# Words of a float64 weight landing in the memory of the other weight, loaded ahead of their rounding

## The chip, the core and the metric

The kernel runs on one core of a Trainium2 chip. The metric is device time in microseconds (us), the median of several executions. TensorE (PE) multiplies matrices, VectorE (DVE) and ScalarE (ACT) work elementwise, SyncE (SP) issues the loads and GpSimd (POOL) the stores. Each engine takes its own instructions strictly in the order in which the program wrote them, and waits for the others by semaphores.

## The reference, cut to what matters

```
B, H, S, Ns, D = 8, 8, 512, 32, 64            # x: (B,H,S,D), state: (B,H,Ns,D), float32
scores  = scale * x @ state^T                  # per batch and head
xread   = softmax(scores) @ state
scores2 = scale * state @ x^T
sread   = softmax(scores2) @ x
t   = concat([xread, sread], axis=2)           # (B,H,544,64) -> (B*544, 512)
h   = t @ w_in                                 # w_in: (512, 2048), float64
g   = h * sigmoid(1.702 * h)
out = g @ w_out                                # w_out: (2048, 512), float64 -> float32
```

Both weights arrive as float64, 8.4 MB each, and the kernel has to round them to float32 itself.

## The kernel before, in words

**Rounding the weights.** The two weights are cut into 32 pieces of 128 rows by 512 float64 numbers (512 KB of words each): pieces 0 to 15 are w_in (four column chunks c of four row blocks k), pieces 16 to 31 are w_out (block f). `load_weight` (L116) brings the words of a piece into a buffer `raw`, of which the pool has three. `round_a` (L142) makes a power of two from the exponent bits: one DVE instruction (L147) and two of ACT (L148, L149). `round_b` (L151) has four DVE instructions (L158 to L161) and writes the float32 piece; it needs the power. `round_next` (L167) does round_a up to two pieces ahead, then one round_b, and then issues the load of the piece three after the one just rounded, since its buffer is now free. A w_in piece is loaded as two transfers of 64 partitions, because heads j and j+4 are paired and their rows of w_in are not neighbours; a chunk c of x takes two transfers for the same reason.

**The batches.** For batch b: `att_state` and `att_xT` transpose state and x on PE with copies on ACT; `att_scores` makes the scores; `att_read_scores`, `att_x_exp`, `att_s_softmax` and `att_x_norm` are the softmaxes on DVE and ACT; `att_eT` and `att_sread` read x by state. `att_M(b, c)` (L269) multiplies state into column chunk c of w_in and needs its four pieces; ACT copies the result M out of PSUM. `up_x(b, f)` (L338) makes 128 of the 2048 columns of h and g (4 PE instructions, then one ACT activation, the gelu); `down` (L352) adds block f of w_out into the output (8 PE instructions for the four token chunks of a batch).

**The order.** All is written out by hand at L368 to L453. First batch 0 and the scores of batch 1, with the first four pieces rounded in between; then `chunk(b, c)`, which is one M and four ups, for (0,0), (0,1), (1,0), (1,1), (0,2), (0,3), most with one piece rounded after each up; then for f = 0 to 15 the down of batch 0 together with the second half of the ups of batch 1, again with one piece after each f. This is called the front below. After it come batches 1 to 7, which need no rounding.

The ups take turns in two PSUM buffers, so an up waits for the gelu of the up before last. PSUM for M, transposes and sread is also two buffers.

Of the kernel before, what the change touches and what calls it, by code (L numbers as in the profile page):

```python
# [10 lines left out]
FP32 = mybir.dt.float32  # L11
I32 = mybir.dt.int32
# [8 lines left out]
def kernel(  # L21
# [26 lines left out]
    nc = tc.nc  # L48

    B, H, S, D = x.shape  # L50
    Ns = state.shape[2]
    DM = H * D
    DF = moe_w_in.shape[1]
    P = 128
    NPR = P // Ns
    NG = H // NPR
    NF = DF // P
    SCH = S // P
    ST = S + Ns
    FC = 512  # L60
    NFC = DF // FC
# [4 lines left out]

    out_x = out.rearrange("(b t) n -> b t n", b=B)[:, :S].rearrange("b (c q) n -> b c q n", c=SCH)
    out_s = out.rearrange("(b t) n -> b t n", b=B)[:, S:]
    x_v = x.rearrange("b (g j) (c q) d -> b c g q j d", g=NG, c=SCH)
    st_v = state.rearrange("b (g j) n d -> b (j n) g d", g=NG)  # L70

    konst = ctx.enter_context(tc.tile_pool(name="konst", bufs=1))
    xpool = ctx.enter_context(tc.tile_pool(name="xpool", bufs=2))
    apool = ctx.enter_context(tc.tile_pool(name="apool", bufs=1))
    mpool = ctx.enter_context(tc.tile_pool(name="mpool", bufs=3))
    wpool = ctx.enter_context(tc.tile_pool(name="wpool", bufs=2))
# [15 lines left out]
    xn, stn = {}, {}  # L92

    def load_state(b):
        stn[b] = apool.tile([P, NG, D], FP32, tag="stn", name=f"stn_{b}", bufs=2)
        nc.sync.dma_start(stn[b], st_v[b])

    def load_x(b):
        xn[b] = xpool.tile([P, SCH, NPR, NG, D], FP32, tag="xn", name=f"xn_{b}")
        for c in range(SCH):  # L100
            for g in range(NG):
                nc.sync.dma_start(xn[b][:, c, :, g], x_v[b, c, g])  # L102

    def x_heads(b, c, j):
        return xn[b][:, c, j].rearrange("q g d -> q (g d)")


    w_in = [konst.tile([P, NPR, FC], FP32, name=f"w_in_{c}") for c in range(NFC)]
    w_out = [konst.tile([P, DM], FP32, name=f"w_out_{f}") for f in range(NF)]
    w_in_words, w_out_words = moe_w_in.bitcast(I32), moe_w_out.bitcast(I32)  # L110
    w_in_rows = w_in_words.rearrange("(g j d) n -> j g d n", g=NG, j=NPR)

    PIECES = [("i", c, k) for c in range(NFC) for k in range(NPR)] + [("o", f) for f in range(NF)]
    raw, power = {}, {}

    def load_weight(i):  # L116
        key = PIECES[i]
        raw[i] = wpool.tile([P, 2 * FC], I32, tag="raw", name="raw_" + "_".join(map(str, key)), bufs=3)
        if key[0] == "i":
            _, c, k = key  # L120
            for g in range(NG):
                nc.sync.dma_start(raw[i][D * g : D * (g + 1)], w_in_rows[k, g, :, 2 * FC * c : 2 * FC * (c + 1)])  # L122
        else:
            f = key[1]
            nc.sync.dma_start(raw[i], w_out_words[P * f : P * (f + 1)])

# [9 lines left out]
    def words(i):  # L138
        w = raw[i].rearrange("p (n w) -> p w n", w=2)
        return w[:, 0].bitcast(U32), w[:, 1]  # L140

    def round_a(i):  # L142

        _, hi = words(i)
        sc = wpool.tile([P, FC], I32, tag="sc", name=f"sc_{i}", bufs=3)
        power[i] = sc
        nc.vector.tensor_scalar(sc, hi, 0x7FF00000, None, ALU.bitwise_and)  # L147
        nc.scalar.activation(out=sc.bitcast(FP32), in_=sc, func=AF.Relu, bias=edge[0], scale=-8.0)  # L148
        nc.scalar.activation(out=sc, in_=sc.bitcast(FP32), func=AF.Relu, bias=edge[1], scale=-1.0)  # L149

    def round_b(i):  # L151
        key = PIECES[i]
        dst = w_in[key[1]][:, key[2]] if key[0] == "i" else w_out[key[1]]
        lo, hi = words(i)
        sc = power.pop(i)

        fr = wpool.tile([P, FC], I32, tag="fr", name=f"fr_{i}")
        nc.vector.tensor_scalar(fr, hi, 0xFFFFF, 0x100000, ALU.bitwise_and, ALU.bitwise_or)  # L158
        nc.vector.scalar_tensor_tensor(sc, hi, -0x80000000, sc, ALU.bitwise_and, ALU.bitwise_or)  # L159
        nc.vector.scalar_tensor_tensor(dst, lo, 2.0**-32, fr, ALU.mult, ALU.add)  # L160
        nc.vector.scalar_tensor_tensor(dst, dst, 2.0**-20, sc.bitcast(FP32), ALU.mult, ALU.mult)  # L161
        del raw[i]

    AHEAD = 2
    done = {"a": 0, "b": 0}

    def round_next(n):  # L167

        for _ in range(n):
            if done["b"] == len(PIECES):  # L170
                return
            while done["a"] < min(done["b"] + 1 + AHEAD, len(PIECES)):
                round_a(done["a"])
                done["a"] += 1
            round_b(done["b"])
            done["b"] += 1
            nxt = done["b"] + 2
            if nxt < len(PIECES):
                load_weight(nxt)

    def w_in_of(k, f):
        c, o = divmod(P * f, FC)
# [12 lines left out]
    def att_state(b):  # L195
        ps = att_ps([P, P], f"stT_{b}")
        nc.tensor.transpose(ps, stn[b].rearrange("p g d -> p (g d)"), ident)  # L197
        A[b]["stT"] = apool.tile([P, P], FP32, tag="stT", name=f"stT_{b}", bufs=2)
        copies(b, 0)(A[b]["stT"], ps)  # L199
# [16 lines left out]
    def att_scores(b):  # L216
        a = A[b]
        a["s"] = [psO.tile([P, S], FP32, tag="o", name=f"s_{b}_{g}") for g in range(NG)]
        by_state(b, a["s"], lambda rows, j: a["xT"][rows, j])
# [17 lines left out]
    def att_s_softmax(b):  # L237

        for e, sm in A[b]["e2"]:
            nc.vector.tensor_scalar(sm, sm, eps, None, ALU.add)  # L240
            nc.vector.reciprocal(out=sm, in_=sm)
            nc.vector.tensor_scalar(e, e, sm, None, ALU.mult)
# [3 lines left out]
    def att_x_exp(b):  # L246

        a = A[b]
        t = a["e1"].rearrange("p g i n -> p (g i) n")
        mx = apool.tile([P, NS1], FP32, tag="mx", name=f"mx_{b}")  # L250
        nc.vector.reduce_max(out=mx, in_=t, axis=AX.X)
        nc.vector.tensor_tensor(out=t, in0=t, in1=mx.to_broadcast((P, NS1, Ns)), op=ALU.subtract)
        nc.scalar.activation(out=t, in_=t, func=AF.Exp, scale=scale)

    def att_x_norm(b):

        a = A[b]
        t = a["e1"].rearrange("p g i n -> p (g i) n")
        sm = apool.tile([P, NS1], FP32, tag="sm", name=f"sm_{b}")
        nc.vector.reduce_sum(out=sm, in_=t, axis=AX.X)  # L260
        nc.vector.tensor_scalar(sm, sm, eps, None, ALU.add)
        nc.vector.reciprocal(out=sm, in_=sm)
        nc.vector.tensor_tensor(out=t, in0=t, in1=sm.to_broadcast((P, NS1, Ns)), op=ALU.mult)
        a["aT"] = apool.tile([P, NG, S], FP32, tag="aT", name=f"aT_{b}", bufs=2)
        nc.vector.transpose(
            a["aT"].rearrange("p g t -> p (g t)"), a["e1"].rearrange("p g i n -> p (g i n)")
        )
# [59 lines left out]
    G = {}  # L327
# [24 lines left out]
    def down(key, r, fs, dst):  # L352

        if fs[0] == 0:
            O[key, r] = psO.tile([P, DM], FP32, tag="o", name=f"o_{key}_{r}")
        ops = O[key, r]
        for f in fs:
            nc.tensor.matmul(  # L358
                ops, G[key, f][:, P * r : P * (r + 1)], w_out[f], start=(f == 0), stop=(f == NF - 1)
            )  # L360
        if fs[-1] == NF - 1:
            osb = opool.tile([P, DM], FP32, tag="osb", name=f"osb_{key}_{r}")
            nc.scalar.copy(osb, ops)  # L363
            nc.gpsimd.dma_start(dst, osb)  # L364

    load_state(0)  # L368
    load_weight(0)
    load_x(0)  # L370
    load_weight(1)
    load_state(1)
    load_weight(2)
    load_x(1)
    att_state(0)
    round_next(1)
    for j in range(NPR):
        att_xT(0, j)
    att_scores(0)
    att_read_scores(0)  # L380
    round_next(1)
    att_x_exp(0)
    att_s_softmax(0)
    att_x_norm(0)
    att_state(1)
    for j in range(NPR):
        att_xT(1, j)
    att_scores(1)
    for g in range(NG):
        att_eT(0, g)  # L390
    att_sread(0)
    round_next(NPR - 2)


    nper = FC // P

    def chunk(b, c, rounds):
        att_M(b, c)
        for f in range(nper * c, nper * (c + 1)):
            up_x(b, f)  # L400
            if rounds:
                round_next(1)

    chunk(0, 0, True)
    att_read_scores(1)
    att_x_exp(1)
    att_s_softmax(1)
    att_x_norm(1)
    chunk(0, 1, True)
    for g in range(NG):  # L410
        att_eT(1, g)
    att_sread(1)
    chunk(1, 0, False)
    chunk(1, 1, True)
    chunk(0, 2, True)
    chunk(0, 3, True)
    load_state(2)
    load_x(2)


    rest = list(range(2 * nper, NF))
    for f in range(NF):
        for r in range(SCH):
            down(0, r, [f], out_x[0, r])
        if f % 2:
            if rest[0] % nper == 0:
                att_M(1, rest[0] // nper)
            up_x(1, rest.pop(0))
        round_next(1)

    nb = P // Ns
    for b in range(1, B):
        ahead = b + 1 < B
# [12 lines left out]
        for u in range(4 * SCH):  # L446
            r, i = divmod(u, 4)
# [36 lines left out]
```

## Time and profile before

| | us |
|---|---|
| median of 3 runs | 945.84 (944.11 to 946.02) |
| the profiled execution | 946.34 |
| its span in the profile | 944.6 |
| PE busy | 844.3 |
| DVE busy | 203.1 |
| ACT busy | 229.1 |

The page's second part cuts the span into 40 slices of 23.6 us and gives each engine's busy share in tenths; the clock that PE was granted is given the same way. PE's busy time has modelled ends, so where it is dense the time between the starts of its instructions is the better measure. The chain of waits goes from the last instruction back to what released each step.

### The profile page before, as it was taken

How to read it: one execution, taken by the hardware profiler on the slowest of the kernel's cores; microseconds unless marked ns; L12 is line 12 of the kernel's file. 1: busy time of each engine (PE TensorE's matmuls, PEld its weight loads, DVE VectorE, ACT ScalarE, POOL GpSimd, SP SyncE). 2: the span in 40 equal slices, each digit the busy share in tenths (PEclk: the TensorE clock that was granted, in tenths of full speed). 3: DMA queues.
4: the chain of work that ended last, by engine and by line, in shares of the span. 5: the costliest groups of instructions: out<-in, count | busy, mean ns of one | idle time of the engine just before them, and what ended most of it. 6: DMA issues, size and time to landing. Idle time of an engine off the chain costs nothing.

```text
span 944.6 us, 6837 instructions
## 1 busy us (share of the span) xinstructions
PE 844.3 (89%) x2824; PEld 392.2 (42%) x2824; DVE 203.1 (22%) x366; ACT 229.1 (24%) x380; POOL 19.7 (2%) x42
## 2 busy tenths in 40 slices
PE   2555384689999999999999999999999999999997
PEld 1312331234443544354435443544354435844443
DVE  1737424444014001500050005000500050000000
ACT  3444244332102130213021302131213121202100
POOL 0000000000000000000000000000000000000000
PEclk9786587889999999999999999999999999999999
DMA  9131212353000200020002000200000000000000
GB/s 183 45 84 50 71 62 99 106 133 70 29 30 12 67 1 14 12 67 0 15 12 67 1 14 12 67 0 12 12 22 1 12 11 20 4 12 12 0 23 23
DMA packets 43967, 35.05 MB, mean 37 GB/s; under 512 B 37664, under 2 KB 37664, under 8 KB 43936
## 3 DMA queue, kind: packets, MB, share of 16 engines
q1 hardware_dynamic: 40832, 25.70, 11.0%
q0 software_dynamic: 3104, 8.92, 2.6%
q8 instruction: 22, 0.36, 0.2%
q14 instruction: 9, 0.07, 0.0%
HBM read 25.69 MB, written 8.91 MB: 37 GB/s over the span
## 4 chain that ended last, share of the span: by engine, by line
issue 66%; PE 15%; DMA 8%; DVE 6%; POOL 2%; SPq 1%; ACT 1%; POOLq 0%; DVEq 0%; ACTq 0%
PE o L358 10%; DMA raw_i<-in_moe_w_in_dram 4%; DMA raw_o<-in_moe_w_out_dram 4%; PE h L333 3%; POOL out_dram L364 2%; DVE sc L159 1%; DVE sc L147 1%; PE M L214 1%; DVE w_in L160 1%; PE sr L293 1%; SPq L122 1%; DVE fr L158 1%; SPq L102 1%; DVE w_out L160 1%; PE xT L206 0%
## 5 line engine op out<-in xcount | busy, mean ns | idle before, releaser
L358 PE MATMUL o<-w_out,g 128*128 128x512 f32 x1024 | 456.2, 595 | 0.0
L358 PEld LDWEIGHTS o<-w_out,g 128*128 128x128 f32 x1024 | 189.0, 190 | 232.8 <-issue 232.1
L333 PE MATMUL h<-aT,M 128*128 128x512 f32 x512 | 233.6, 612 | 35.0 <-ACT M L276 35.0
L333 PEld LDWEIGHTS h<-aT,M 128*128 128x128 f32 x512 | 98.9, 196 | 169.4 <-issue 115.0
L335 ACT ACTIVATE g<-h 128x512 f32<-128x512 f32 x128 | 76.1, 595 | 141.1 <-PE h L333 141.1
L214 PE MATMUL M<-w_in,stT 64*32 64x512 f32 x512 | 45.0, 622 | 16.4 <-DVE w_in L161 16.4
L276 DVE COPY M<-M 128x512 f32<-128x512 f32 x24 | 16.4, 682 | 194.6 <-PE M L214 194.6
L363 ACT COPY osb<-o 128x512 f32<-128x512 f32 x32 | 18.7, 585 | 135.2 <-PE o L358 132.9
L293 PE MATMUL sr<-eT,xn 128*128 128x64 f32 x256 | 33.0, 292 | 18.5 <-ACT eT L286 18.5
L148 ACT ACTIVATE sc<-sc,edge 128x512 f32<-128x512 int32 x32 | 23.0, 720 | 81.3 <-DVE sc L147 81.2
L206 PE MATMUL xT<-ident,xn 128*128 128x128 f32 x128 | 22.9, 310 | 21.9 <-ACT stT L199 8.1
L293 PEld LDWEIGHTS sr<-eT,xn 128*128 128x128 f32 x256 | 32.9, 209 | 21.9 <-ACT eT L286 19.0
L276 ACT COPY M<-M 128x512 f32<-128x512 f32 x40 | 22.5, 584 | 68.2 <-PE M L214 68.2
L364 POOL DMA_DIRECT2D out_dram<-osb x32 | 17.5, 546 | 866.4 <-ACT osb L363 866.3
L206 PEld LDWEIGHTS xT<-ident,xn 128*128 128x128 f32 x128 | 18.2, 161 | 36.5 <-issue 14.6
L207 ACT COPY xT<-xT 128x512 f32<-128x512 f32 x20 | 11.6, 584 | 88.3 <-PE xT L206 88.3
L333 PE MATMUL h_sr<-srT,w_in 128*128 128x256 f32 x128 | 27.8, 379 | 0.0
L358 PE MATMUL o_sr<-w_out,g_sr 128*128 128x512 f32 x64 | 27.6, 592 | 0.0
L199 DVE COPY stT<-stT 128x128 f32<-128x128 f32 x6 | 1.7, 291 | 119.8 <-PE stT L197 119.8
L214 PEld LDWEIGHTS M<-w_in,stT 64*32 64x32 f32 x512 | 7.5, 106 | 46.1 <-issue 22.7
L333 PEld LDWEIGHTS h_sr<-srT,w_in 128*128 128x128 f32 x128 | 24.3, 190 | 3.7 <-issue 0.5
L149 ACT ACTIVATE sc<-sc,edge 128x512 int32<-128x512 f32 x32 | 23.1, 722 | 1.1
(52 smaller groups left out, 306.0 us busy)
## 6 DMA issues: line engine op xcount, KB each, us to landing
raw_i<-in_moe_w_in_dram SPq DMA_DIRECT2D x32, 256.0 KB, 4.2
xn<-in_x_dram SPq DMA_DIRECT2D x64, 128.0 KB, 3.4
raw_o<-in_moe_w_out_dram SPq DMA_DIRECT2D x16, 512.0 KB, 3.3
out_dram<-osb POOLq DMA_DIRECT2D x32, 256.0 KB, 2.3
stn<-in_state_dram SPq DMA_DIRECT2D x8, 64.0 KB, 2.0
out_dram<-osb_sr POOLq DMA_DIRECT2D x2, 256.0 KB, 7.1
```

What stands on the lines that cost most here:

```text
L148: nc.scalar.activation(out=sc.bitcast(FP32), in_=sc, func=AF.Relu, bias=edge[0], scale=-8.0)
L149: nc.scalar.activation(out=sc, in_=sc.bitcast(FP32), func=AF.Relu, bias=edge[1], scale=-1.0)
L160: nc.vector.scalar_tensor_tensor(dst, lo, 2.0**-32, fr, ALU.mult, ALU.add)
L206: nc.tensor.transpose(ps[:, c], x_heads(b, c, j), ident)
L214: nc.tensor.matmul(ps[g][st], A[b]["stT"][rows, st], rhs(rows, j), start=True, stop=True)
L276: copies(b, g)(m[:, g], ps[g])
L293: nc.tensor.matmul(ps[:, j], x_heads(b, c, j), a["eT"][:, :, c, Ns * j : Ns * (j + 1)], start=(c == 0), stop=(c == SCH - 1),)
L333: nc.tensor.matmul(hps, lhs[i], rhs[i], start=(i == 0), stop=(i == n - 1))
L335: nc.scalar.activation(out=gt, in_=hps, func=AF.Gelu_apprx_sigmoid)
L358: nc.tensor.matmul(ops, G[key, f][:, P * r : P * (r + 1)], w_out[f], start=(f == 0), stop=(f == NF - 1))
L363: nc.scalar.copy(osb, ops)
L364: nc.gpsimd.dma_start(dst, osb)
```

## The change

Order and memory of the front change; no arithmetic is added or left out.

- Heads 2j and 2j+1 are paired, so a w_in piece and a chunk of x are one transfer each (x: 4 instead of 8 per batch); state becomes two transfers.
- w_out becomes one tile of 16 blocks. The words of pieces 0 to 7 land in it (two blocks hold one piece), and those of pieces 12 to 15 again in its first eight blocks. Pieces 8 to 11 and all of w_out use the pool, now with four buffers.
- Loads are issued apart from the rounding: eight pieces at the start, and from the fifth rounded piece on eight ahead of the rounding (`load_weights`, `powers_to`, `round_to`).
- The order of the first batches: fewer powers ahead at the start, `att_x_norm(0)` after the scores of batch 1; in the chunks `pace` spreads the pieces: one per up in chunk (0,0), none in (0,1), three per chunk in the next four, then 1.5 per f.

```diff
-    x_v = x.rearrange("b (g j) (c q) d -> b c g q j d", g=NG, c=SCH)
+    x_v = x.rearrange("b h (c q) d -> b c q h d", c=SCH)
...
-    w_out = [konst.tile([P, DM], FP32, name=f"w_out_{f}") for f in range(NF)]
+    w_out = konst.tile([P, NF, DM], FP32, name="w_out")
...
+        nin, room = NFC * NPR, NF // 2
+        if i < room or nin - NPR <= i < nin:
+            o = 2 * (i % room if i < room else i - (nin - NPR))
+            raw[i] = w_out[:, o : o + 2].rearrange("p f n -> p (f n)").bitcast(I32)
+        else:
+            raw[i] = wpool.tile([P, 2 * FC], I32, tag="raw", name="raw_" + "_".join(map(str, key)), bufs=4)
...
+    def powers_to(n):
+        while done["a"] < min(n, len(PIECES)):
+            load_weights(done["a"] + 1)
+            round_a(done["a"])
+            done["a"] += 1
+    def round_to(n, ahead=AHEAD):
+        while done["b"] < min(n, len(PIECES)):
+            powers_to(done["b"] + 1 + ahead)
+            round_b(done["b"])
+            done["b"] += 1
+            if done["b"] > NPR:
+                load_weights(done["b"] + 2 * NPR)
+    def pace(pieces):
+        done["credit"] += pieces
+        n = int(done["credit"])
+        done["credit"] -= n
+        round_to(done["b"] + n)
...
-    chunk(0, 1, True)
+    chunk(0, 1, 0)
...
-    chunk(1, 0, False)
-    chunk(1, 1, True)
-    chunk(0, 2, True)
-    chunk(0, 3, True)
+    chunk(1, 0, 3)
+    chunk(1, 1, 3)
+    chunk(0, 2, 3)
+    chunk(0, 3, 3)
```

SP's queue at the start of the program, before and then after (`raw_i` is the pool's buffer of a w_in piece, `xn` and `stn` are x and state of one batch):

```order
L96 DMA stn_117<-in_state_dram 128x2x64
L122 DMA raw_i_0_119<-in_moe_w_in_dram 64x1024 x2
L102 DMA xn_122<-in_x_dram 128x4x64 x8
L122 DMA raw_i_1_131<-in_moe_w_in_dram 64x1024 x2
L96 DMA stn_134<-in_state_dram 128x2x64
L122 DMA raw_i_2_136<-in_moe_w_in_dram 64x1024 x2
L102 DMA xn_139<-in_x_dram 128x4x64 x8
L122 DMA raw_i_3_169<-in_moe_w_in_dram 64x1024 x2
```

```order
L129 DMA w_out<-in_moe_w_in_dram 128x1024
L97 DMA stn_103<-in_state_dram 128x1x64 x2
L102 DMA xn_106<-in_x_dram 128x8x64 x4
L129 DMA w_out<-in_moe_w_in_dram 128x1024 x3
L97 DMA stn_114<-in_state_dram 128x1x64 x2
L102 DMA xn_117<-in_x_dram 128x8x64 x4
L129 DMA w_out<-in_moe_w_in_dram 128x1024 x4
L129 DMA raw_i_0_339<-in_moe_w_in_dram 128x1024
L129 DMA raw_i_1_341<-in_moe_w_in_dram 128x1024
L129 DMA raw_i_2_343<-in_moe_w_in_dram 128x1024
L129 DMA raw_i_3_345<-in_moe_w_in_dram 128x1024
```

The fourth piece had to wait for the first to be rounded; now eleven pieces stand behind the first with no rounding between them.

ACT at the start, before and then after (`sc` is a power, `stT` and `xT` the transposed state and x of batch 0):

```order
L199 COPY stT_150<-stT_148 128x128
L148 ACTIVATE sc_152<-sc_152,edge_112 128x512
L149 ACTIVATE sc_152<-sc_152,edge_114 128x512
L148 ACTIVATE sc_156<-sc_156,edge_112 128x512
L149 ACTIVATE sc_156<-sc_156,edge_114 128x512
L148 ACTIVATE sc_160<-sc_160,edge_112 128x512
L149 ACTIVATE sc_160<-sc_160,edge_114 128x512
L207 COPY xT_172<-xT_0_173 128x512
L207 COPY xT_172<-xT_1_179 128x512
```

```order
L152 ACTIVATE sc_126<-sc_126,edge_97 128x512
L153 ACTIVATE sc_126<-sc_126,edge_99 128x512
L216 COPY stT_137<-stT_135 128x128
L224 COPY xT_139<-xT_0_140 128x512
L224 COPY xT_139<-xT_1_146 128x512
```

The powers of pieces 1 and 2 stood ahead of the copies of batch 0's transposes; now only that of piece 0 does.

ACT in chunk (1,0), before and then after (`M` is the product of state and w_in, `g` the gelu of an up):

```order
L276 COPY M_0_572<-M_0_0_573 128x512
L276 COPY M_0_572<-M_0_1_574 128x512
L335 ACTIVATE g_0_588<-h_0_585 128x512
L335 ACTIVATE g_1_593<-h_1_590 128x512
L335 ACTIVATE g_2_598<-h_2_595 128x512
L335 ACTIVATE g_3_603<-h_3_600 128x512
L276 COPY M_1_605<-M_1_0_606 128x512
L276 COPY M_1_605<-M_1_1_607 128x512
```

```order
L293 COPY M_0_490<-M_0_0_491 128x512
L293 COPY M_0_490<-M_0_1_492 128x512
L352 ACTIVATE g_0_506<-h_0_503 128x512
L352 ACTIVATE g_1_511<-h_1_508 128x512
L152 ACTIVATE sc_513<-sc_513,edge_97 128x512
L153 ACTIVATE sc_513<-sc_513,edge_99 128x512
L352 ACTIVATE g_2_527<-h_2_524 128x512
L152 ACTIVATE sc_529<-sc_529,edge_97 128x512
L153 ACTIVATE sc_529<-sc_529,edge_99 128x512
L352 ACTIVATE g_3_543<-h_3_540 128x512
L152 ACTIVATE sc_545<-sc_545,edge_97 128x512
L153 ACTIVATE sc_545<-sc_545,edge_99 128x512
```

Three powers now stand among the four gelus of this chunk, the last of them ahead of the copies of the next M.

## Rows read from the trace of the kernel before

**Rows 1.** The page, 40 slices of the span: PE's busy share in tenths.

```profile
PE   2555384689999999999999999999999999999997
```

**Rows 2.** Busy time by stretch: span, us and instructions of each engine, granted clock, DMA share, GB/s.

```profile
120.70:258.20 137.50, 108.85 (x305) 45.44 (x306) 49.80 (x93) 45.48 (x73) 1.22 (x2) 0.90 0.28 81
258.20:944.60 686.40, 680.88 (x2295) 318.97 (x2293) 96.73 (x168) 138.64 (x234) 17.71 (x32) 1.00 0.06 19
```

**Rows 3.** The chain of waits, a w_in piece: start, us, engine or transfer, tile, line.

```profile
40.51 4.52 DMA raw_i<-in_moe_w_in_dram
...
47.67 4.31 DMA raw_i<-in_moe_w_in_dram
```

**Rows 4.** The chain of waits, a w_out piece.

```profile
147.40 3.35 DMA raw_o<-in_moe_w_out_dram
...
152.84 3.04 DMA raw_o<-in_moe_w_out_dram
```

**Rows 5.** Instructions in order of time, first 20 us: start, us, engine, line [idle before].

```profile
12.57 1.30 PE L206 MATMUL xT<-ident,xn 128*128 128x128 f32 x5 [1.67 <-DMA xn<-in_x_dram]
...
17.85 0.72 ACT L148 ACTIVATE sc<-sc,edge 128x512 f32<-128x512 int32 x1 [1.14 <-DVE sc L147]
...
19.23 1.05 ACT L207 COPY xT<-xT 128x512 f32<-128x512 f32 x2
```

**Rows 6.** Busy time by stretch: x and w_in loading together.

```profile
9.00:18.50 9.50, 2.23 (x7) 1.30 (x7) 1.54 (x4) 2.31 (x4) 0.00 (x0) 1.00 1.17 211
```

**Rows 7.** DVE in order of time: batch 0's softmaxes with one piece between.

```profile
24.44 0.69 DVE L229 TENSOR_REDUCE mx<-s 128x1 f32<-128x512 f32 x1 [4.36 <-PE s L214]
...
27.25 0.38 DVE L147 TENSOR_SCALAR sc<-raw_i 128x512 int32<-128x512 int32 x1
...
29.82 1.21 DVE L251 TENSOR_REDUCE mx<-e 128x32 f32<-128x1024 f32 x1
...
33.77 1.21 DVE L260 TENSOR_REDUCE sm<-e 128x32 f32<-128x1024 f32 x1
...
38.05 0.39 DVE L147 TENSOR_SCALAR sc<-raw_i 128x512 int32<-128x512 int32 x1
```

**Rows 8.** PE in order of time: sread of batch 0 and 1, then ups.

```profile
40.81 3.79 PE L293 MATMUL sr<-eT,xn 128*128 128x64 f32 x32 [0.73 <-ACT eT L286]
...
110.32 7.09 PE L293 MATMUL sr<-eT,xn 128*128 128x64 f32 x32 [17.79 <-ACT eT L286]
...
120.70 8.88 PE L333 MATMUL h<-aT,M 128*128 128x512 f32 x16 [0.71 <-ACT M L276]
...
163.92 9.45 PE L333 MATMUL h<-aT,M 128*128 128x512 f32 x16 [13.05 <-ACT M L276]
```

**Rows 9.** ACT in order of time: a gelu, and the next one with a power between.

```profile
133.35 0.60 ACT L335 ACTIVATE g<-h 128x512 f32<-128x512 f32 x1 [1.58 <-PE h L333]
...
135.21 0.58 ACT L335 ACTIVATE g<-h 128x512 f32<-128x512 f32 x1
```

**Rows 10.** In order of time: from batch 1's softmax to the up behind it.

```profile
75.40 0.68 DVE L229 TENSOR_REDUCE mx<-s 128x1 f32<-128x512 f32 x1
...
82.41 9.25 PE L333 MATMUL h<-aT,M 128*128 128x512 f32 x16 [4.96 <-ACT M L276]
```

**Rows 11.** The chain of waits in the downs of batch 0.

```profile
228.73 1.13 PE M L214 x16
...
230.48 1.98 PE h L333 x4
232.46 6.87 PE o L358 x16
239.33 1.72 PE h L333 x4
```

**Rows 12.** Busy time by stretch: PE dense, PE waiting, PE dense after a long wait.

```profile
138.40:142.50 4.10, 1.08 (x18) 0.17 (x17) 2.43 (x5) 3.06 (x6) 0.00 (x0) 1.00 0.21 83
...
163.90:168.50 4.60, 4.58 (x6) 2.00 (x7) 1.92 (x5) 1.22 (x3) 0.00 (x0) 0.50 0.34 114
```

More of the change, by code (lines that the diff above doesn't have):

```diff
@@ L68 @@
     out_s = out.rearrange("(b t) n -> b t n", b=B)[:, S:]
-    x_v = x.rearrange("b (g j) (c q) d -> b c g q j d", g=NG, c=SCH)
-    st_v = state.rearrange("b (g j) n d -> b (j n) g d", g=NG)
+    x_v = x.rearrange("b h (c q) d -> b c q h d", c=SCH)
+    st_v = state.rearrange("b (j g) n d -> b g j n d", g=NG)
     konst = ctx.enter_context(tc.tile_pool(name="konst", bufs=1))
@@ L95, in load_state @@
         stn[b] = apool.tile([P, NG, D], FP32, tag="stn", name=f"stn_{b}", bufs=2)
-        nc.sync.dma_start(stn[b], st_v[b])
+        for g in range(NG):
+            nc.sync.dma_start(stn[b][:, g], st_v[b, g])
     def load_x(b):
-        xn[b] = xpool.tile([P, SCH, NPR, NG, D], FP32, tag="xn", name=f"xn_{b}")
+        xn[b] = xpool.tile([P, SCH, H, D], FP32, tag="xn", name=f"xn_{b}")
         for c in range(SCH):
-            for g in range(NG):
-                nc.sync.dma_start(xn[b][:, c, :, g], x_v[b, c, g])
+            nc.sync.dma_start(xn[b][:, c], x_v[b, c])
     def x_heads(b, c, j):
-        return xn[b][:, c, j].rearrange("q g d -> q (g d)")
+        return xn[b][:, c, NG * j : NG * (j + 1)].rearrange("q g d -> q (g d)")
     w_in = [konst.tile([P, NPR, FC], FP32, name=f"w_in_{c}") for c in range(NFC)]
-    w_out = [konst.tile([P, DM], FP32, name=f"w_out_{f}") for f in range(NF)]
+    w_out = konst.tile([P, NF, DM], FP32, name="w_out")
     w_in_words, w_out_words = moe_w_in.bitcast(I32), moe_w_out.bitcast(I32)
-    w_in_rows = w_in_words.rearrange("(g j d) n -> j g d n", g=NG, j=NPR)
     PIECES = [("i", c, k) for c in range(NFC) for k in range(NPR)] + [("o", f) for f in range(NF)]
@@ L117, in load_weight @@
         key = PIECES[i]
-        raw[i] = wpool.tile([P, 2 * FC], I32, tag="raw", name="raw_" + "_".join(map(str, key)), bufs=3)
+        nin, room = NFC * NPR, NF // 2
[4 more added lines that the diff above has]
+            raw[i] = wpool.tile([P, 2 * FC], I32, tag="raw", name="raw_" + "_".join(map(str, key)), bufs=4)
         if key[0] == "i":
             _, c, k = key
-            for g in range(NG):
-                nc.sync.dma_start(raw[i][D * g : D * (g + 1)], w_in_rows[k, g, :, 2 * FC * c : 2 * FC * (c + 1)])
-        else:
-            f = key[1]
-            nc.sync.dma_start(raw[i], w_out_words[P * f : P * (f + 1)])
+            src = w_in_words[P * k : P * (k + 1), 2 * FC * c : 2 * FC * (c + 1)]
+        else:
+            src = w_out_words[P * key[1] : P * (key[1] + 1)]
+        nc.sync.dma_start(raw[i], src)
     least, most = float((1023 - 127) << 20), float((1023 + 128) << 20)
@@ L152, in round_b @@
         key = PIECES[i]
-        dst = w_in[key[1]][:, key[2]] if key[0] == "i" else w_out[key[1]]
+        dst = w_in[key[1]][:, key[2]] if key[0] == "i" else w_out[:, key[1]]
         lo, hi = words(i)
@@ L164, with load_weights @@
     AHEAD = 2
[L165 to L174, printed above, removed]
+    done = {"load": 0, "a": 0, "b": 0, "credit": 0.0}
+    def load_weights(upto):
+        while done["load"] < min(upto, len(PIECES)):
+            load_weight(done["load"])
+            done["load"] += 1
+    def powers_to(n):
[6 more added lines that the diff above has]
+            powers_to(done["b"] + 1 + ahead)
             round_b(done["b"])
             done["b"] += 1
-            nxt = done["b"] + 2
-            if nxt < len(PIECES):
-                load_weight(nxt)
+            if done["b"] > NPR:
[5 more added lines that the diff above has]
+        round_to(done["b"] + n)
     def w_in_of(k, f):
@@ L358, in down @@
             nc.tensor.matmul(
-                ops, G[key, f][:, P * r : P * (r + 1)], w_out[f], start=(f == 0), stop=(f == NF - 1)
+                ops, G[key, f][:, P * r : P * (r + 1)], w_out[:, f], start=(f == 0), stop=(f == NF - 1)
             )
@@ L364, in down @@
             nc.gpsimd.dma_start(dst, osb)
+    load_weights(1)
     load_state(0)
-    load_weight(0)
     load_x(0)
-    load_weight(1)
+    load_weights(NPR)
     load_state(1)
-    load_weight(2)
     load_x(1)
+    load_weights(2 * NPR)
+    round_to(1, 0)
     att_state(0)
-    round_next(1)
     for j in range(NPR):
@@ L380 @@
     att_read_scores(0)
-    round_next(1)
+    powers_to(2)
     att_x_exp(0)
+    round_to(2, 1)
     att_s_softmax(0)
-    att_x_norm(0)
     att_state(1)
@@ L388 @@
     att_scores(1)
+    att_x_norm(0)
+    powers_to(4)
     for g in range(NG):
@@ L391, with chunk @@
     att_sread(0)
-    round_next(NPR - 2)
+    round_to(NPR, 1)
     nper = FC // P
-    def chunk(b, c, rounds):
+    def chunk(b, c, pieces):
+        round_to(NPR * (c + 1))
         att_M(b, c)
@@ L400, in chunk @@
             up_x(b, f)
-            if rounds:
-                round_next(1)
-    chunk(0, 0, True)
+            pace(pieces / nper)
+    chunk(0, 0, NPR)
     att_read_scores(1)
@@ L422 @@
     for f in range(NF):
+        round_to(NFC * NPR + f + 1)
         for r in range(SCH):
@@ L428 @@
             up_x(1, rest.pop(0))
-        round_next(1)
+        pace(1.5)
     nb = P // Ns
```

## The prediction

> **What bounds the kernel now.** I read the slices of the page first. PE's row shows 3 to 8 tenths for about eight slices, then 9 to the end [rows 1]. So there are two stages, and the table by stretch prices them: from 258.2 us on PE is busy 680.9 of 686.4 us and nothing there can give much; ahead of 258.2, the front, is where the kernel loses time, and even its last part, 120.7 to 258.2, has only 108.9 us of PE in 137.5 [rows 2]. I write T for the end of the front, 258.2 now. Whatever moves T moves the end by as much, since the rest is PE's own work.
>
> Next the chain of waits inside the front. It alternates between loads of weight words and DVE: one load begins at 40.51, takes 4.52, and the next load on the chain begins at 47.67 [rows 3]; so a w_in piece costs 7.16 us, of which the load and its issue are well over half. For w_out the period is 152.84 - 147.40 = 5.44 us [rows 4]. The reason stands in the code: with three buffers the load of piece n+3 waits for piece n to be rounded, and the power of n+3, which waits for that load, stands ahead of the rounding of n+1 on DVE. Load and rounding take turns. Rounding alone takes DVE 29.82 - 27.25 = 2.57 us for a piece [rows 7], 2.65 with the gaps I allow. So 32 pieces are 85 us of DVE work, spread over about 215 us.
>
> **The change, step by step.** I follow the program to the start of the first up of batch 1 (now 120.70 [rows 8]), and then to T.
>
> Step 1, start. Piece 0, state and x of batch 0 are 1.64 MB. Now the last chunk of x lands for the transposes at 12.57, but ACT copies nothing until 19.23, because the power of piece 2 stands ahead, and piece 2 landed only shortly before 17.85 [rows 5]. With that order gone, x decides. At 211 GB/s, seen when x and w_in load together [rows 6], 1.64 MB are 7.8 us with no start-up at all; 12.57 is the other bound; I take 10.5, between them. From the first copy to the start of DVE on the scores it is now 24.44 - 19.23 = 5.2 us [rows 5, 7]; with 0.8 more, as no transposes are done in advance, DVE starts at 16.5 instead of 24.44.
>
> By the Trainium skill (SBUF — State Buffer, Summary: rules for kernel authors) one should reckon HBM loads at about 358 GB/s. The trace does not agree for this stretch: 211 GB/s with the DMA share above 1 [rows 6]. By the Trainium skill the 1.64 MB would take 4.6 instead of 7.8 us, and the time would be 3 us below mine, 871; by the row it is 874.
>
> Step 2, DVE of batch 0. In after's order: score reading 27.25 - 24.44 = 2.8; piece 1 and the first part of piece 2, 2.9; exponent and state softmax 33.77 - 29.82 = 3.95; normalisation 38.05 - 33.77 = 4.3 [rows 7]; pieces 2 and 3, 5.3. Sum 19.25, so piece 3 is done at 35.7. The normalisation ends at 30.5.
>
> Step 3, to the first up. ACT does the power of piece 3 (30.9 to 32.3) and the copies of eT (to 33.5); then sread on PE takes 3.79 or 7.09 us, as it meets a fast or a slow clock [rows 8]; then srT copies, the power of piece 4 and the first M copy, 2.7 together. The first up begins at 40.0 (fast) or, with M at the slow clock too, about 44.
>
> Step 4, chunk (0,0). Here ACT's queue sets the pace: gelu 0, powers 5 and 6, gelu 1, power 7 and so on. An up is 1.72 us [rows 11], or 3.4 at half the clock; a gelu with one power is 135.21 - 133.35 = 1.86 [rows 9]. Power 5 is ready at 40 + 1.72 + 1.86 = 43.6, or 49.3; from then DVE needs 2.0 for the rest of piece 5 and 2 x 2.65 for 6 and 7. Piece 7 is done at 50.9 or 56.6. The softmax of batch 1 follows, which DVE starts at 75.40 now [rows 10]. No load is in this chain: pieces up to 11 are issued at the start, and 7.4 MB up to piece 9 take 35 us at 211 GB/s, so they land before their turn.
>
> Step 5, to the first up of batch 1. From batch 1's softmax to the next up it is 82.41 - 75.40 = 7.0 us [rows 10], with the same instructions after. Chunk (0,1) now rounds nothing; its four ups start at a slow clock after a wait, 9.45 as at 163.92 [rows 8]. Then eT and its copies 1.8, sread 3.8, copies, M and its copy 2.2: 7.8. Sum 24.3: the first up of batch 1 begins at 75.2 or 80.9 instead of 120.70.
>
> Step 6, to T. Chunks (1,0), (1,1), (0,2), (0,3). Four ups are 4 x 1.72 = 6.9 of PE, and M with its first copy 230.48 - 228.73 = 1.75 [rows 11]: 8.65 a chunk if PE alone counts. But three powers now stand among the gelus, the last ahead of M's copies: 3.44 for two ups, 3 x 1.86 on ACT, 0.65 for the copy, 9.65. That is a cost of 1.0 in each of three chunks. Then the downs: two f with an up are 6.87 + 1.72 = 8.59 [rows 11], eight times, with two M of 1.75: 72.2. Together 3 x 9.65 + 6.9 + 72.2 = 108.1. DVE needs 2.65 for a piece and PE takes one block in 4.3, so I cost rounding at nothing there: PE's downs hide it. If that cover were gone, see the first rival.
>
> T is 183.3 or 189.0, a gain of 74.9 or 69.2. The span becomes 869.7 or 875.4. The profiled execution took 1.7 more than its span, and 0.5 more than the median of the runs: 870.9 to 876.6 as a median. I take **874**, the middle.
>
> The other edits cost nothing on this path. State takes two issues instead of one, but x takes four instead of eight on the same queue. The waits added on SP (pieces 12 to 15 for the rounding of 0 to 3, later ones for a pool buffer) hold back only loads behind them; pieces 0 to 3 are done by 35.7, and x of batch 2, which stands behind piece 27, is first read after T. After T all engines have the same instructions, so the 686.4 stay.
>
> **The rivals.**
>
> Tail set by rounding. If the four pool buffers still make load and rounding take turns at 5.44 [rows 4], the sixteen w_out pieces need 87 us from about 97 on (piece 15), the last is ready at 184, and its down and up end 5.2 later: T 189 to 195, time 877 to 883. For it: the buffers rotate still. Against: with a fourth one, two pieces' rounding and not one covers a load of 3.3. Chance 0.08.
>
> The head start ends with the memory. If from piece 8 on each piece costs 7.16 again [rows 3] and each w_out piece 5.44, piece 15 comes at about 62 + 57 = 119, piece 31 at 206, T is 211, time 898. It is also the case that the change does not do what it says beyond the first eight. Against: pieces 8 to 15 wait for nothing that is late. Chance 0.10, with other stalls of 15 to 30 us on ACT's queue that I have not seen.
>
> Quicker than reckoned: x early, no clock loss in step 5 (9.45 becomes 6.9), chunks at 8.65: 3 + 2.5 + 3 off the fast case, 862 to 866. Chance 0.05.
>
> The clock, the slower side. PE was granted half its clock (0.50, 1.2 GHz) at 163.9, after it had waited 13.05 us [rows 8, 12]. If PE stayed at half through all of step 6, its 4 x 6.9 + 68.7 of dense work would take 96 us more: T about 282, time 971. It decides once more than 72 us of that work run at half. Against: across 138.4 to 142.5, where PE was busy 1.08 of 4.10 us, the clock stayed at 1.00 [rows 12], and step 6 leaves shorter waits than that, under 3 us. Chance 0.03.
> The Trainium skill (TensorE: Matmul & The Clock Gate, Part 1) says that the slow clock is PE's default and that only activity releases it; the two rows agree with it, and by it shorter waits are a second gain, which the fast case above contains.
>
> **How the numbers follow.** Forecast 874, own range 866 to 881, chance 0.74. The range that should hold 8 in 10 takes in the quick case and the first rival, and reaches part of the way to the second: 860 to 892. Faster by over 0.2% (about what a measurement of this kernel can tell from no change) has all but the clock rival and a little: 0.96; same 0.01; slower 0.03.
>
> **What would show it right or wrong.** After: the copies of batch 0's transposes on ACT near 10.5, not 19; first up at 40 to 44; batch 1's softmax on DVE at 51 to 57; the first up of batch 1 at 75 to 81; dense PE, clock 1.00, from there; T at 183 to 189. DVE's waits for `raw` loads (the period of rows 3 and 4) should be nearly gone. Wrong would be a chain that still alternates between loads and DVE, a PE clock of 0.5 in step 6, or a stretch after T longer than 686.4.

## The result, and the profile after

The changed kernel takes 875.95 us (median of 4 runs, 875.02 to 878.31) beside 945.93 for the kernel before on the same chip: a ratio of 0.927, interval 0.924 to 0.929. 874 was forecast. One run of e3 (1121.41 us) and one of e6 (4980.77 us) below were slow runs; they are outside the ranges and ratios given there, though counted in the two medians.

The page of the changed kernel, 40 slices of its span of 875.1 us: PE's busy share and the clock it was granted, in tenths.

```profile
PE   4769799999999999999999999999999999999997
PEclk9589999999999999999999999999999999999999
```

PE was thin for about eight slices [rows 1]; now the low digits are 4, 7, 6 and one more 7, all in the first five slices, and the clock is low in the second and third alone. The table by stretch of the changed kernel (span, us and instructions of PE, PEld, DVE, ACT and POOL, granted clock, DMA share, GB/s):

```profile
79.06:188.69 109.63, 102.83 (x305) 43.32 (x306) 57.38 (x106) 49.81 (x81) 1.22 (x2) 1.00 0.30 93
188.69:875.10 686.41, 680.89 (x2294) 318.96 (x2293) 96.77 (x168) 138.96 (x234) 17.79 (x32) 1.00 0.07 19
```

They answer to [rows 2]. The stretch after the front is 686.41 us, 686.40 before. All of the gain is in T: 188.69 instead of 258.2, 69.5 us. The first up of batch 1 begins 41.6 earlier (79.06, not 120.70), and from there to T takes 109.6 instead of 137.5, 27.9 less.

What DVE waited for in the front (what waited, for what: us in total, times, longest), the kernel before and then the changed one:

```profile
DVE sc L147 <- DMA raw_i<-in_moe_w_in_dram: 58.8, 13, 7.2
...
DVE sc L147 <- DMA raw_o<-in_moe_w_out_dram: 45.7, 16, 3.7
```

```profile
DVE sc L163 <- ACT sc L153: 32.3, 8, 12.0
DVE sc L151 <- DMA w_out<-in_moe_w_in_dram: 5.1, 1, 5.1
...
DVE sc L151 <- DMA raw_o<-in_moe_w_out_dram: 4.5, 1, 4.5
```

29 waits for words, 104.5 us, have become two of 9.6 together: one for the very first piece, and one during the downs, where the chain does not pass through DVE. What DVE waits for now are the powers on ACT. The longest of these waits, 12.0, ends at 84.79: since nothing is paced in chunk (0,1), ACT makes no power between 54.8 and 83.3, and DVE stops when the powers made earlier are used up. The turn-taking of [rows 3, 4] is gone.

PE in order of time between the copies of x and the first up of batch 1, the changed kernel (start, us, engine, line, operation, count, [idle before and what ended it]):

```profile
9.74 3.12 PE L223 MATMUL xT<-ident,xn 128*128 128x128 f32 x13 [0.47 <-DMA xn<-in_x_dram]
...
32.02 7.09 PE L310 MATMUL sr<-eT,xn 128*128 128x64 f32 x32 [2.31 <-ACT eT L303]
39.04 2.65 PE L231 MATMUL M<-w_in,stT 64*32 64x512 f32 x16
42.43 6.87 PE L350 MATMUL h<-aT,M 128*128 128x512 f32 x12 [0.74 <-ACT M L293]
...
62.30 8.89 PE L350 MATMUL h<-aT,M 128*128 128x512 f32 x16 [5.83 <-ACT M L293]
...
72.85 3.79 PE L310 MATMUL sr<-eT,xn 128*128 128x64 f32 x32 [0.78 <-ACT eT L303]
```

Sread met the slow clock at 32.02 (7.09 us, [rows 8] has both sizes), and so did M behind it (2.65, and 1.78 elsewhere in this trace) and the four ups at 62.30.

### The profile page after: what moved, and what is told of

The parts are those of the page before. It is cut to its first block, busy times and chain, and to the rows that moved or that the text cites. A ratio compares the mean times of both kernels' runs of the same rounds, so it can differ in the third digit from the quotient of the medians.

```text
span 875.1 us, 6754 instructions
## 1 busy us (share of the span) xinstructions
PE 835.9 (96%) x2824; PEld 389.8 (45%) x2824; DVE 203.4 (23%) x366; ACT 227.8 (26%) x380; POOL 19.8 (2%) x42
## 4 chain that ended last, share of the span: by engine, by line
issue 71%; PE 20%; ACT 3%; DVE 3%; POOL 2%; DMA 1%; SPq 0%; POOLq 0%; ACTq 0%
PE o L375 11%; PE h L350 5%; POOL out_dram L381 2%; PE sr L310 1%; PE M L231 1%; ACT sc L153 1%; ACT sc L152 1%; ACT g L352 1%; PE xT L223 1%; DMA xn<-in_x_dram 1%; ACT M L293 0%; PE s L231 0%; DVE w_in L165 0%; DVE e L248 0%; DVE sc L163 0%
## 5 line engine op out<-in xcount | busy, mean ns | idle before, releaser
L350 PE MATMUL h<-aT,M 128*128 128x512 f32 x512 | 228.9, 602 | 14.6 <-ACT M L293 14.1
L231 PE MATMUL M<-w_in,stT 64*32 64x512 f32 x512 | 41.2, 615 | 1.7 <-DVE w_in L165 1.7
L223 PEld LDWEIGHTS xT<-ident,xn 128*128 128x128 f32 x128 | 17.9, 158 | 24.5 <-issue 12.6
L350 PEld LDWEIGHTS h_sr<-srT,w_in 128*128 128x128 f32 x128 | 24.3, 190 | 3.7 <-issue 0.5
L224 DVE COPY xT<-xT 128x512 f32<-128x512 f32 x12 | 8.3, 692 | 63.8 <-PE xT L223 63.8
```

The costliest lines, as they stand in the source:

```text
L223: nc.tensor.transpose(ps[:, c], x_heads(b, c, j), ident)
L224: copies(b, j)(A[b]["xT"][:, j], ps.rearrange("p c q -> p (c q)"))
L231: nc.tensor.matmul(ps[g][st], A[b]["stT"][rows, st], rhs(rows, j), start=True, stop=True)
L350: nc.tensor.matmul(hps, lhs[i], rhs[i], start=(i == 0), stop=(i == n - 1))
```

## The experiments

All times are medians; each kernel ran beside the kernel before, whose medians were 945.93 to 946.60.

| kernel | us | range | ratio, interval |
|---|---|---|---|
| changed | 875.95 | 875.02 to 878.31 | 0.927 (0.924 to 0.929) |
| e1: order new, loads old | 916.28 | 915.14 to 916.72 | 0.968 (0.966 to 0.970) |
| e2: order old, loads new | 892.04 | 890.56 to 892.49 | 0.942 (0.940 to 0.944) |
| e8: head start of 8 pieces only | 910.30 | 909.92 to 911.69 | 0.962 (0.961 to 0.964) |
| e3: heads paired as before | 878.63 | 878.13 to 880.13 | 0.928 (0.926 to 0.930) |
| e4: pieces on the first ups | 873.58 | 872.01 to 874.29 | 0.923 (0.921 to 0.925) |
| e5: powers ahead of sread | 871.49 | 871.06 to 872.61 | 0.921 (0.920 to 0.922) |
| e6: 42 idle transposes | 871.64 | 871.13 to 877.74 | 0.923 (0.920 to 0.925) |
| e9: 58 idle transposes | 873.36 | 872.94 to 874.18 | 0.924 (0.922 to 0.925) |
| e7: softmax of batch 1 early | 864.35 | 863.98 to 867.68 | 0.914 (0.913 to 0.916) |
| e10: e7 mended | 863.40 | 862.78 to 863.97 | 0.913 (0.911 to 0.914) |

**The two halves of the change.** e1 keeps the new order and pairing and gives the loads back their pool of three:

```diff
-        if i < room or nin - NPR <= i < nin:
-            raw[i] = w_out[...]
...
-            raw[i] = wpool.tile([P, 2 * FC], I32, ..., bufs=4)
+        raw[i] = wpool.tile([P, 2 * FC], I32, ..., bufs=3)
...
-            if done["b"] > NPR:
-                load_weights(done["b"] + 2 * NPR)
+            load_weights(done["b"] + 3)
...
-    load_weights(NPR)
+    load_weights(3)
...
-    load_weights(2 * NPR)
```

> The changed kernel's order and pairing, but the loads as in the kernel before: every piece goes through a pool of three buffers and the load of piece n+3 is issued when piece n is rounded. Theory (loads that run ahead of the rounding carry a good part of the gain): from piece 5 on load and rounding take turns again, about 5.4 us for a piece; piece 7 is done at about 63 instead of 55.4 us, piece 31 at about 202, the front ends near 207 instead of 188.7, time 890 to 900. Rival (order and pace of the first batches carry it, the loads were hidden or nearly): 876 to 880.

e2 is the kernel before, order, pace and pairing, with the loads in w_out's memory and eight ahead:

> The kernel before with one part of the change: words land in w_out's memory and loads run eight pieces ahead; its order, its pace and its pairing of heads (two transfers for a piece) stay. Theory (both parts count): the start stays as before, first up near 50 us, piece 7 near 62, first up of batch 1 near 90 instead of 79 us, time 883 to 893. Rival 1 (loads ahead are all of it): 875 to 879. Rival 2 (order is nearly all of it): over 920.

The loads alone gain 946.6 - 892.0 = 54.6 us, the order (with the pairing) alone 30.3, both 70. They overlap by 15, so each is worth less when the other is there; that the order hides some of the waiting for loads is the likely reason. e2 fell inside the range of its theory; its ACT shows what the order is for at the start. The copies of batch 0's transposes behind the powers, e2:

```profile
18.32 0.72 ACT L154 ACTIVATE sc<-sc,edge 128x512 int32<-128x512 f32 x1
18.95 1.05 ACT L215 COPY xT<-xT 128x512 f32<-128x512 f32 x2
```

18.95 is where before had 19.23 [rows 5]; the changed kernel's first such copy after x has landed is at 10.25. e1 went the way of its theory but was 16 us slower than its upper end, which e8 explains.

**The head start alone.** e8 lets only pieces 0 to 7 land in w_out and sends the other 24 through a pool of three. It is the second rival built as a kernel.

```diff
-        if i < room or nin - NPR <= i < nin:
+        if i < room:
...
-                load_weights(done["b"] + 2 * NPR)
+                load_weights(max(2 * NPR + 3, done["b"] + 3))
```

> The changed kernel with only the first eight pieces in w_out's memory; all others go through a pool of three buffers, each load issued when the piece three before it is rounded. This is the second rival of the prediction. Theory (it is the run-ahead beyond eight pieces that lets rounding keep pace with the later chunks and the downs): from piece 11 on about 5.4 us for a piece, piece 31 near 195 or later, time 890 to 915. Rival (the head start of eight is what counts): 876 to 882.

It took 910.3, inside the theory's wide range, but the price of the prediction's rival was 898. Its chain of waits, around the last piece of w_out:

```profile
181.02 3.27 DMA raw_o<-in_moe_w_out_dram
...
186.38 3.27 DMA raw_o<-in_moe_w_out_dram
...
190.21 0.73 ACT sc L152
...
190.96 0.72 ACT sc L153
191.68 0.48 ACT g L352
192.16 0.48 ACT M L293
...
192.69 3.78 PE h L350 x4
196.47 8.14 PE o L375 x16
```

The period is 186.38 - 181.02 = 5.36, the 5.44 of [rows 4] again. The price was low for another reason. Pieces are paced at 1.5 for each f, so the power of the last piece stands on ACT ahead of the copies of the last M of batch 1; the up at 192.69 had waited 12.14 us for these copies by the same trace. Three more pairs of f, each two downs (16 PE instructions) and an up, come behind it, so T is 223.5 instead of the 211 of the rival. This is so although the last piece is rounded at 197.0, earlier than the 206 of the rival. A late load does not only delay its own down: it delays everything that stands behind its power on ACT. e1 shows the same, with an up at 198.81 that waited 13.26 us for the copies of M. The changed kernel has the same pace, and its longest wait for copies of M in step 6 is 1.78 us; so loads that run ahead are what makes the new pace safe.

**The pairing.** e3 pairs heads j and j+4 again, and so loads a w_in piece and a chunk of x as two transfers each.

```diff
-    x_v = x.rearrange("b h (c q) d -> b c q h d", c=SCH)
+    x_v = x.rearrange("b (g j) (c q) d -> b c g q j d", g=NG, c=SCH)
...
-        nc.sync.dma_start(raw[i], src)
+            for g in range(NG):
+                nc.sync.dma_start(raw[i][D * g : D * (g + 1)], w_in_rows[k, g, :, ...])
```

> The changed kernel with heads j and j+4 paired as before: two transfers of 64 partitions for a w_in piece and two for a chunk of x, state in one. Theory (the single transfers matter only where a load is waited for, at the start): x of batch 0 lands at about 12.5 instead of 9.7 us, everything behind shifts by 2 to 3, time 877 to 879. Rival (a piece in two halves takes 4.2 instead of 3.3 us to land, and that counts for each of 16 w_in pieces): 885 to 890.

878.63 against 875.95: the intervals of the ratios overlap (0.926 to 0.930 and 0.924 to 0.929). At most the pairing is worth a few us. The time lies in the range of the theory, 877 to 879, but only times were compared, so its step, the later landing of x, is not shown. The rival, 885 to 890, is out.

**The pace in the chunks.** The prediction charged 1.0 us for each of three chunks because the last of three powers stands ahead of the copies of M. ACT in chunk (1,0) of the changed kernel:

```profile
82.80 0.60 ACT L352 ACTIVATE g<-h 128x512 f32<-128x512 f32 x1 [1.12 <-PE h L350]
83.29 0.71 ACT L152 ACTIVATE sc<-sc,edge 128x512 f32<-128x512 int32 x1
84.04 0.72 ACT L153 ACTIVATE sc<-sc,edge 128x512 int32<-128x512 f32 x1
84.66 0.58 ACT L352 ACTIVATE g<-h 128x512 f32<-128x512 f32 x1
...
87.74 0.72 ACT L153 ACTIVATE sc<-sc,edge 128x512 int32<-128x512 f32 x1
88.37 1.06 ACT L293 COPY M<-M 128x512 f32<-128x512 f32 x2
```

e4 puts the three pieces of a chunk behind its first three ups:

```diff
-            pace(pieces / nper)
+            if pieces == nper or f % nper < pieces:
+                pace(1 if pieces else 0)
```

> The changed kernel with the three pieces of a chunk rounded after its first three ups instead of its last three, so that no power stands ahead of the copies of the next M on ScalarE. Theory (that order is what stretches a chunk from 8.7 to 9.9 us): three chunks become 8.9 each, time 872 to 874. Rival (ScalarE's total work binds these chunks, its order does not matter): unchanged, 875 to 877.

PE in the same chunks of e4:

```profile
78.77 7.13 PE L350 MATMUL h<-aT,M 128*128 128x512 f32 x16 [0.71 <-ACT M L293]
85.84 1.09 PE L231 MATMUL M<-w_in,stT 64*32 64x512 f32 x16
87.66 7.13 PE L350 MATMUL h<-aT,M 128*128 128x512 f32 x16 [0.73 <-ACT M L293]
```

A chunk takes 87.66 - 78.77 = 8.89 us, 9.93 in the changed kernel: 1.04 each, as charged, and PE's wait for M falls from 1.78 to 0.73. The downs begin 3.4 us earlier (112.44, 115.83 in the changed kernel). The median fell by 2.4 us; the intervals of the two ratios just overlap.

**The slow clock ahead of sread.** Before sread at 32.02 PE had waited 2.31 us, because ACT made a power ahead of the copies of eT. e5 puts the copies ahead of that power:

```diff
-    powers_to(4)
     for g in range(NG):
         att_eT(0, g)
-    att_sread(0)
+    powers_to(4)
     round_to(NPR, 1)
+    round_to(NPR + 1)
+    att_sread(0)
...
-    chunk(0, 0, NPR)
+    chunk(0, 0, NPR - 1)
```

> The changed kernel with the eT copies ahead of the power of piece 3, and the powers of pieces 3 to 6 and the rounding of pieces 2 to 4 ahead of batch 0's sread, while ScalarE waits for TensorE there. Theory (the chain from 39 to 62 us runs over ScalarE's queue: powers 4 to 7 stand behind srT, M and gelu, and VectorE waits 5.9 and 3.9 us for them): piece 7 is done near 48 instead of 55.4 us, the next up starts near 55 instead of 62.3, time 867 to 871. Rival (VectorE's or TensorE's own work sets this stretch): 874 to 876.

PE in e5:

```profile
30.36 3.79 PE L310 MATMUL sr<-eT,xn 128*128 128x64 f32 x32 [0.73 <-ACT eT L303]
34.07 1.04 PE L231 MATMUL M<-w_in,stT 64*32 64x512 f32 x2
38.10 1.79 PE L231 MATMUL M<-w_in,stT 64*32 64x512 f32 x14 [2.99 <-ACT srT L319]
```

With 0.73 us of waiting sread takes 3.79, not 7.09. Part of it goes again at once: M waits 2.99 us for srT, whose copies now stand behind two powers, and the four ups behind it run at the slow clock (9.39 us from 40.59 on). Piece 7 was rounded at 50.6 and the next up began at 57.53, where the theory had 48 and 55. The median fell by 4.5 us, to 0.5 above the theory's range.

That kernel changes the order of the work too. e6 and e9 leave the order and give PE transposes of the identity to do, whose result is not used: 24 among the transposes of batch 1's x, and 18 or 34 ahead of sread.

```diff
     for j in range(NPR):
+        if j == 1:
+            warm(24, 0)
         att_xT(1, j)
...
         att_eT(0, g)
+    warm(34, 1)
     att_sread(0)
```

> The changed kernel with added transposes of the identity into an unread PSUM tile, 24 ahead of batch 1's second xT and 18 ahead of batch 0's sread, where TensorE waits 3.8 and 2.3 us. Nothing reads them. Theory (sread and M of batch 0 ran at half the clock because TensorE had waited, and that is the difference between my fast and my slow case): sread takes 3.8 instead of 7.1 us, the first up begins near 37 to 39 instead of 42.4, time 869 to 873. Rival (the clock there does not hang on these waits, or what it gives is lost behind ScalarE): 875 to 878.

> The changed kernel with work added that is not used: 24 transposes of the identity on PE among the transposes of batch 1's x, and 34 (18 in the earlier run of this kind) between the transposes of eT and sread, so that PE's wait for the copies of eT is filled. Clock theory (sread takes 7.09 instead of 3.79 us because PE has waited 2.31 us before it): sread takes 3.8 us in the profile with a granted clock of 1.00 and begins near 32; the first M and ups follow at the full clock, the first up of batch 1 comes about 5 us earlier (74) and the median is 869 to 872. Rival (something other than PE's waiting, such as the weight words loading beside it, sets sread's pace): sread stays near 7 us and the median at 875 to 877.

The profile of e6 is of the run of 877.74 us; the three others in its range took 871.1 to 871.6. In the profile 18 transposes were too few, and PE still waited 1.90 us and ran at half the clock. PE in e6, and then in e9:

```profile
28.54 2.13 PE L388 MATMUL warm<-ident 128*128 128x128 f32 x18
32.57 6.85 PE L310 MATMUL sr<-eT,xn 128*128 128x64 f32 x32 [1.90 <-ACT eT L303]
39.36 2.65 PE L231 MATMUL M<-w_in,stT 64*32 64x512 f32 x16
```

```profile
29.36 3.88 PE L388 MATMUL warm<-ident 128*128 128x128 f32 x34
33.07 3.68 PE L310 MATMUL sr<-eT,xn 128*128 128x64 f32 x32
36.69 1.78 PE L231 MATMUL M<-w_in,stT 64*32 64x512 f32 x16
39.48 5.42 PE L350 MATMUL h<-aT,M 128*128 128x512 f32 x12 [1.02 <-ACT M L293]
...
57.91 9.16 PE L350 MATMUL h<-aT,M 128*128 128x512 f32 x16 [5.83 <-ACT M L293]
```

By the table of stretches the clock in e9 is 1.00 over 32.0 to 35.0 us and 35.0 to 39.5, and 0.50 in the changed kernel in both. Sread and M take 5.5 us together instead of 9.7, although the weight words load beside them as before; so it is the waiting of PE, not the loading, that sets their pace. Of the two waits that e9 fills, of 3.79 us at 23.41 and of 2.31 ahead of sread, the second decides: in e6 the first was filled and the second only shortened to 1.90, and sread stayed slow; in e5 the first stayed (3.25 us) and the second fell to 0.73, and sread was quick. The first up of batch 1 begins at 74.94, 4.1 earlier. The four ups at 57.91 still run slow, behind the same wait of 5.83. The median, 873.36, lies 1.4 above the range of the theory, though the steps in the trace came nearly as it said (the profiled runs differ by 3.9 us, 876.84 and 872.94, the medians by 2.6); why three runs of e6 were another 2 us quicker than e9 stays open, since no trace of them is there.

**A quicker version.** After chunk (0,0) PE waits 5.83 us while DVE and ACT do the whole softmax of batch 1, and earlier DVE waits 5.85 and 3.87 us for powers. e7 has e4's edit and the copies of eT ahead of the power, as e5. It fills DVE's waits with the first half of batch 1's softmax, and does the rest beside the ups of chunk (0,1):

```diff
...
+    powers_to(NPR + 2)
+    att_read_scores(1)
     att_sread(0)
+    att_x_exp(1)
...
     chunk(0, 0, NPR)
-    att_read_scores(1)
-    att_x_exp(1)
+    chunk(0, 1, 0)
     att_s_softmax(1)
     att_x_norm(1)
-    chunk(0, 1, 0)
...
```

> The changed kernel with batch 1's score reading and exponent moved ahead into the stretch where VectorE waits (35 to 41 us), eT copies and powers up to piece 5 ahead of sread, batch 1's normalisation behind chunk (0,1), and the pieces of a chunk on its first ups. Theory (batch 1's softmax stood between piece 7 and the next up, with two table loads on ScalarE): M of chunk (0,1) near 50, its ups from about 52 instead of 62.3 us, first up of batch 1 near 67 instead of 79, time 858 to 863. Rival (ScalarE's total work in chunk (0,0) takes back what is moved): 866 to 872.

It took 864.35 us, 11.6 below the changed kernel and a little above the theory's range. In it M of the first chunk waited 3.56 us for srT's copies, behind a power and two exponents on ACT. e10 moves these behind sread (`att_read_scores(1)` after `att_sread(0)`, `att_x_exp(1)` after the first M):

> The version with the softmax of batch 1 moved forward, mended in the place where it waited: there M of the first chunk waited 3.56 us for the copies of srT, which stood on ACT behind a power and two exponents of batch 1. Here sread stands ahead of the score reading of batch 1, the power of the fifth piece behind it, and the last exponent of batch 1 stands behind the copies of the first M. Theory (only the order on ACT held M back): M waits under 1.5 us, the first up begins at 38 to 39.5 instead of 42.0, and the median is 1 to 3 us below 864.4, at 861 to 863.5. Rival (DVE's rounding of pieces 4 to 7 ends last in any case, since DVE had work without a gap from 30 to 53): the first up comes earlier but the second chunk begins as before near 54, and the median is 863.5 to 865.

PE in e7, and then in e10:

```profile
39.05 1.96 PE L231 MATMUL M<-w_in,stT 64*32 64x512 f32 x14 [3.56 <-ACT srT L319]
42.03 8.94 PE L350 MATMUL h<-aT,M 128*128 128x512 f32 x16 [1.03 <-ACT M L293]
...
54.35 7.13 PE L350 MATMUL h<-aT,M 128*128 128x512 f32 x16 [0.67 <-ACT M L293]
```

```profile
33.88 1.78 PE L231 MATMUL M<-w_in,stT 64*32 64x512 f32 x16
38.39 6.98 PE L350 MATMUL h<-aT,M 128*128 128x512 f32 x12 [2.73 <-ACT M L293]
...
51.51 1.05 PE L231 MATMUL M<-w_in,stT 64*32 64x512 f32 x4 [1.70 <-DVE sm L257]
53.23 7.13 PE L350 MATMUL h<-aT,M 128*128 128x512 f32 x16 [0.67 <-ACT M L293]
```

The first up came 3.6 us earlier as the theory said, but the second chunk only 1.1, and the median fell by 0.95; the intervals of the two ratios overlap. So the rival has the mechanism in the main: with ACT's order mended, the rounding of pieces 4 to 7 on DVE ends last (the L257 that released M is the instruction right behind it), and from 29 to 51.5 us DVE waits only 0.67. In e7 DVE had not worked without a gap, as the expectation has it, but had waited 1.44 us for a power, which gives part of the 1.1. The median lies at the seam of the two ranges, 861 to 863.5 and 863.5 to 865, and does not tell them apart. 863.4 is the best version that was run, 0.913 of the kernel before.

## Why the prediction was right, step by step

| step | forecast | measured |
|---|---|---|
| 1. x landed; DVE starts on the scores | 10.5; 16.5 | 9.74; 15.16 |
| 2. piece 3 rounded | 35.7 | 34.3 |
| 3. sread; first up | 3.79 or 7.09; 40.0 or 44 | 7.09; 42.43 |
| 4. piece 7 rounded | 50.9 or 56.6 | 55.3 |
| 5. first up of batch 1 | 75.2 or 80.9 | 79.06 |
| 6. a chunk; the downs; T | 9.65; 72.2; 183.3 or 189.0 | 9.93; 72.70; 188.69 |
| after T | 686.4 | 686.4 |

Step 1 was forecast 0.8 too late on the landing and 1.3 on DVE. DVE's work of step 2 came as summed (19.1 us for 19.25). For x of batch 0 the row [rows 6] gave the 10.5 of the sum, and 9.74 was measured. By the Trainium skill (SBUF — State Buffer, Summary: rules for kernel authors) one should reckon loads from HBM at about 358 GB/s. Where weight words load alone the trace comes near it: 373 GB/s from 20 to 30 us; from 10 to 20, with x among them for much of it, it was 285. By the Trainium skill's figure x would have landed at 7.3 us, an estimate (10.5 less the 3.2 between 7.8 and 4.6), so the row was the better guide there.

Steps 3 to 5 had two cases and the forecast stood in the middle; the prediction did not say which would come. The slow one came, and e5, e6 and e9 show what decided it, PE's wait of 2.31 us ahead of sread, which comes from the power of piece 3 that the sum itself put ahead of the copies of eT: 7.09 for sread, 2.65 for M, and chunk (0,0) took 12.9 us against 12.6. From batch 1's softmax to its first up it was 23.8 against 24.3, with the four slow ups at 8.89. The slow case alone gave 876.6. That 875.95 lies so near to it is in part luck: the first up of batch 1 came 1.8 us early and step 6 took 1.5 longer, and the two nearly cancel.

In step 6 the mechanism was right and e4 priced it at 1.04. The chunk was 0.28 longer because the second gelu starts 3.74 after the first up, where 3.44 for two ups was reckoned. The downs' chain has the rows of [rows 11] again:

```profile
126.59 6.87 PE o L375 x16
133.45 1.72 PE h L350 x4
```

Rounding was costed at nothing there, and the chain holds no DVE and no load from 115.99 to T. So the first rival (a tail set by rounding) did not happen with four buffers and eight loads ahead; with three, in e1 and e8, load and rounding took turns again. The second rival was under-priced by 12 us, as e8 showed: the price took the last piece to hold only its own down. Its 7.16 for a w_in piece was also the longest of the periods in the kernel before, which run from 6.81 to 7.16. The clock rival (its 971 should be 970 by its own sum) did not come: from 79 us on the clock is 1.00. But the argument against it, that waits under 3 us leave the clock alone, does not hold in these runs: the clock was 0.50 behind 2.31 us ahead of sread, and in e2 behind 1.90 us ahead of four ups. That the 1.78 us waits of step 6 did not cost the clock is in part luck.

What was missed is the room that was left. The step sum followed ACT's queue through chunk (0,0) without asking whether its order could be better. e10 lies 12.5 us below the changed kernel, of which the pace alone (e4) accounts for 2.4.

## What to carry to other kernels

Memory that is empty until late (here the place of a weight that is needed last) can serve as landing room and take the waiting of loads on buffers off the path; here that was worth 54.6 us under the old order and 40.3 under the new one, so gains of this kind should not be added up. On an engine that works in strict order, ask of every instruction what stands behind it: a power for a weight needed much later held up the copies that PE wanted next, by 1 us for a chunk here and by 12 us when its load was late. When a queue is loosened, price the next bound before moving more: e10 took 3.6 us from one wait and kept 1.

## What the runs showed of the hardware

- Sread of batch 0, the same 32 matrix multiplications, took 3.79 us after PE had waited 0.73 us (e5, e7, e10), 3.68 after none (e9), 6.85 after 1.90 (e6) and 7.09 after 2.31 (the changed kernel). The granted clock was 1.00 under the 3.68 and 3.79, and 0.50 under the 6.85 and 7.09. So a far shorter wait than the 13.05 us of [rows 8] was followed by the slow clock. The length of the last wait alone does not decide it: four ups in the kernel before ran at a clock of 1.00 after 3.02 us, and four in e2, behind 1.90, ran at 0.50 from 113.5 to 116.5 (the two rows, in this order):

```profile
142.50 7.36 PE L333 MATMUL h<-aT,M 128*128 128x512 f32 x16 [3.02 <-ACT M L276]
```

```profile
112.54 8.83 PE L341 MATMUL h<-aT,M 128*128 128x512 f32 x16 [1.90 <-ACT M L284]
```

- Useless work on PE went with a faster kernel: 58 transposes of the identity, 8.8 us of PE time, went with a median 2.6 us lower (the intervals of the two ratios just overlap).
- Weight words loaded at 373 GB/s with nothing else on the queues, and at 285 in the ten us before, partly with x among them. In e8 a w_in piece as one transfer has a period of 98.33 - 92.30 = 6.03 us through a pool of three; as two half transfers, in the kernel before, it was 6.81 to 7.16.
